# Gathers held back, PSUM output banks set apart, two lists turned later, two decays on another engine

## The chip, the core and the metric

The kernel runs on one core of a Trainium2 chip. The core has a matrix engine (TensorE, PE in the profile; its weight loads are PEld), three others that compute (VectorE, DVE; ScalarE, ACT; GpSimd, POOL), an engine that only issues transfers (SyncE, SP), and sixteen DMA engines that all transfers share, whichever queue they were issued on. Each engine works through its own instructions in the order in which they were written and waits on semaphores for the others. The metric is the device time of one execution in microseconds; less is better.

## What is computed

Linear attention with a decay per head, and then a layer of experts of which each token uses one. Batch 2, 8 heads, 768 steps, head size 64; 8 experts with a hidden size of 1024.

```python
for t in range(S):                                   # attention
    state = gamma * state + outer(k[:, :, t], v[:, :, t])
    y[:, :, t] = scale * einsum(q[:, :, t], state)
x = y, heads side by side                            # 2 x 768 tokens of 512
for each token s of a batch:                         # experts
    fresh = argmax(x @ w_gate)
    e = fresh if s == 0 or sigmoid(x @ w_local) < 0.5 else prev_e
    p = softmax(x @ w_gate)
    out = p[e] * (relu(x @ w1[e]) @ w2[e])
```

## The kernel before

**Attention** goes through six blocks of 128 steps for both batches. Of each block the keys (and for two blocks at a time the queries) are multiplied by powers of the decay (`decay_k`, `decay_q`), turned by TensorE, copied out of PSUM (`k_evac`, `q_evac`), and used for scores, values and a running state. The rows of x go to a DRAM tensor `xs`, each as 1,024 fp16 numbers (512 high parts and 512 low parts; 2,048 bytes). Routing (`fresh`, `choose`, `carry`, `place`) gives for each expert the list of its tokens.

**Experts.** An expert takes up to 256 tokens, as a first list of 128 and a second list with the rest (112 for expert 0 and so on down; sizes in `CAPS`). Expert 0 is the fixed one (`FEW = 1`): its place and its weights are known before routing ends. The other seven come in the order of how many tokens they have, so that their weights can be loaded only when the ranks are known (`experts`). For a list, GpSimd starts a `gather` (an indirect DMA of rows of `xs` into `xg`, of which there are four buffers), TensorE turns it in 8 transposes (`list_transpose`, tokens lt) into a PSUM tile `xtr`, ScalarE or VectorE copies that to `xx` (`list_evac`, le). Then come 8 up products of 12 matmuls each (`up`), the relu in two parts, `hh` by ScalarE and `hl` by VectorE (`relu`, re), and 8 down products (`down`, dn). Expert 0 is done in two rounds, its first list (up.f.0, dn.f.0) and then its second (up.f.1, dn.f.1); its first result is copied out of PSUM by `hold` (ho). After that a loop over the experts 1 to 7 follows, in which the tokens that are written after the word `late` in `ORDER` are worked off one by one.

**Weights** are loaded as 64 transfers of 512 KB (`load_unit`, into a ring of 18 buffers `stg`), four for w1 and four for w2 of an expert, in that order. Each holds two blocks, and each block is split into an fp16 high part `hi` by ScalarE (`split_hi`, token wh) and a low part `lo` by VectorE (`split_lo`, wl).

**The order** of the whole first half is written out by hand in the string `ORDER`, where each token is one step; each engine gets its part in that order. In the stretch of which the prediction speaks most, after the token `reopen`, stand the second list of expert 0 (lt.0.1, le.0.1, up.0.1 to dn.7.1), the two lists of expert 1 (lt.1.0, lt.1.1 and their copies) and the splits of expert 1's w1 (wh and wl). `reopen` closes the PSUM pool of the attention part (tags `big`, 2 x 2 banks, and `one`, 3 banks) and opens the pool `pn` of the expert part, whose tags `xt` (2), `h` (2) and `o` (3) take the banks over. A new tile then waits for what last used its bank. `warm` issues matmuls on zeros, whose results nobody reads.

Of the kernel before, what the change touches and what calls it, by code (L numbers as in the profile page):

```python
# [9 lines left out]
F32 = mybir.dt.float32  # L10
F16 = mybir.dt.float16
# [7 lines left out]
P = 128  # L19
# [39 lines left out]
ls.0 sc.1.0 er.0.0.a er.0.1.v tk.2 rs.0.2.a mk.1.0 Y.1 ek.2.0.a dq.1.0.p ek.2.1.a av.1.0 av.1.1 dq.1.1.v tq.1.0
xh.1 W W tq.1.1 eq.1.0.0.v W eq.1.0.1.a eq.1.1.1.v sc.2.0 eq.1.1.0.a xl.1 st.2 mk.2.0 dk.3.0.p rt.1.1 lo.1 sn.2  # L60
Y.2 ls.1 fr.0 dk.3.1.p fr.0 fr.0 fr.0 sc.2.1 ch.0 ch.0 ch.0 ch.0 tk.3 mk.2.1 kr.0 ek.3.0.a av.2.0 ke.0 ek.3.1.v
av.2.1 dk.4.0.v tr.0 xh.2 st.3 ca.0 xl.2 dk.4.1.p tc.0 rt.1.0 tk.4 er.1.0.a sn.3 sc.3.1 oh.0 rhs.0 dq.2.0.p
ek.4.0.a er.1.1.v co.0 rs.1.2.a mk.3.1 rt.2.0 ek.4.1.a lo.2 er.2.0.a ls.2 tq.2.0 dq.2.1.p pl.0 pl.0 pl.0 sc.3.0
eq.2.0.0.a eq.2.0.1.v mk.3.0 sc.4.0 es.0 tq.2.1 eq.2.1.1.v Y.3 eq.2.1.0.a mk.4.0 av.3.0 dk.5.0.p pl.0 av.3.1
pl.0 pl.0 dk.5.1.v fi.0 xh.3 tk.5 ad.0 sc.4.1 xl.3 ek.5.0.a ek.5.1.a rt.2.1 mk.4.1 lo.3 er.2.1.a rt.3.1 ls.3
sc.5.0 fr.1 wh.a fr.1 fr.1 ch.1 ch.1 kr.1 ch.1 rs.2.2.a ch.1 rt.3.0 wl.v ke.1 er.3.0.a er.3.1.v tr.1 sc.5.1 ca.1
rs.3.2.a mk.5.0 tc.1 wh.a st.4 wh.a oh.1 wl.v wh.a co.1 wl.v wh.a Y.4 es.1 pl.1 wh.a sn.4 wh.a pl.1 rhs.1 pl.1
av.4.0 wh.a pl.1 pl.1 wh.a pl.1 av.4.1 mk.5.1 wh.a fi.1 xh.4 Y.5 ad.1 early wl.v wh.a wl.v av.5.0 wh.a wl.v
av.5.1 wh.a xl.4 wh.a tot xh.5 rc rt.4.0 wl.v lo.4 er.4.0.a xl.5 rt.4.1 er.4.1.a lo.5 ls.4 wl.v rt.5.0 rs.4.2.a
ls.5 fr.2 rt.5.1 fr.2 er.5.0.a fr.2 ch.2 kr.2 wl.v lt.0.0 ch.2 ke.2 ch.2 ch.2 er.5.1.a le.0.0.v tr.2 ca.2 up.0.0  # L70
rs.5.2.a wl.v wh.a tc.2 up.1.0 oh.2 wh.a rhs.2 wl.v co.2 up.2.0 pl.2 es.2 pl.2 pl.2 up.3.0 pl.2 pl.2 up.4.0 pl.2
re.3.0 fi.2 tot up.5.0 rank ad.2 rank up.6.0 rank rank lists dn.0.0 up.7.0 second experts dn.1.0 wl.v re.7.0 W
dn.2.0 ga W dn.3.0 wl.v W ga wl.v W dn.4.0 wl.v W dn.5.0 wl.v W dn.6.0 W dn.7.0 W ho reopen lt.0.1 lt.1.0
le.0.1.v wh.a wh.a wl.v up.0.1 wh.a wl.v up.1.1 le.1.0.a wl.v up.2.1 wh.a lt.1.1 wh.a wl.v up.3.1 wh.a wl.v
up.4.1 re.3.1 up.5.1 le.1.1.a up.6.1 wl.v wh.a up.7.1 wh.a wl.v dn.0.1 wl.v re.7.1 dn.1.1 dn.2.1 dn.3.1 dn.4.1
dn.5.1 dn.6.1 dn.7.1 late ga ga prob prob prob prob prob prob prob prob prob prob sidx pt pl2 so.1 so.0 rest
rest rest
"""

C_ID = 0  # L80
# [40 lines left out]
def moe_kernel(ctx: ExitStack, tc, q, k, v, w_gate, w_local, w1, w2, cst, out):  # L121
# [245 lines left out]
    with ExitStack() as both:  # L367
# [41 lines left out]
        def decay_q(g, b, eng="p"):  # L409

            T["qs", g, b] = ap_.tile([P, 2, H, D], F32, tag="qs", name=f"qs{g}_{b}", bufs=2)
            src = T["q", g, b].rearrange("t h (two d) -> t h two d", two=2)
            for two in range(2):
                eng_[eng[two % len(eng)]].tensor_tensor(
                    T["qs", g, b][:, two].rearrange("t (j r) d -> t r j d", r=2),
                    src[:, :, two].rearrange("t (r j) d -> t r j d", r=2),
                    qtab[:, g, :, two].rearrange("t (r j) -> t r j", r=2).unsqueeze(3).to_broadcast([P, 2, R, D]),
                    ALU.mult,
                )
# [697 lines left out]
```

## Time and profile before

| | us |
|---|---|
| median of 3 runs | 239.21 |
| lowest and highest of them | 237.76 and 239.99 |
| the profiled execution, its own time | 238.68 |
| its span, from the first to the last instruction | 236.9 |
| TensorE busy in the span | 216.7 (91%) |
| VectorE, ScalarE, GpSimd busy | 156.8, 135.4, 55.0 |

The span is 1.8 us shorter than the profiled execution's time. All times in rows are counted from the start of the span. In a list of instructions the number in brackets at the end of a row is the idle time of that engine just before, and what ended it.

### The profile page before, as it was taken

What the parts mean: (1) busy time and instruction counts of PE and PEld (TensorE: products, weight loads), DVE (VectorE), ACT (ScalarE), POOL (GpSimd) and SP (SyncE); (2) the same over time, 40 slices, a digit from 0 to 9 for tenths busy, and PEclk for the clock granted to TensorE, in tenths of its full rate; (3) what the DMA queues carried; (4) which work ended last, traced back from release to release, by engine and by line L of the source; (5) the groups of instructions that cost most, each with busy time, mean ns of one, the idle gap of its engine ahead of it and who ended that gap; (6) DMA issues with size and microseconds to landing.
All of it is one profiled execution on the core that took longest, in us unless ns stands there. A gap on an engine that the chain in (4) does not pass through costs nothing. (4 is left out here: it accounts for less than half of the span.)

```text
span 236.9 us, 7289 instructions
## 1 busy us (share of the span) xinstructions
PE 216.7 (91%) x3056; PEld 178.1 (75%) x3056; DVE 156.8 (66%) x312; ACT 135.4 (57%) x234; POOL 55.0 (23%) x69
## 2 busy tenths in 40 slices
PE   7699898999879859999999999999999999999960
PEld 2489797988779356786589869959969969959940
DVE  2659597889988655188877647756846956967500
ACT  2224415368871257066656676876786886877420
POOL 2334236402102630000111333333021242011030
PEclk9999999999979999999999999999999999999997
DMA  7999999989632699999999896899768622001001
GB/s 168 275 163 266 263 229 256 265 251 400 231 134 79 200 338 358 387 387 386 387 391 335 254 326 209 288 313 291 257 200 284 240 88 74 0 12 44 7 14 44
DMA packets 54565, 53.85 MB, mean 227 GB/s; under 512 B 28516, under 2 KB 34788, under 8 KB 54528
## 3 DMA queue, kind: packets, MB, share of 16 engines
q1 hardware_dynamic: 49952, 43.41, 60.1%
q0 software_dynamic: 2944, 6.78, 8.7%
q10 hardware_dynamic: 1632, 3.15, 3.6%
q8 instruction: 25, 0.41, 0.8%
q14 instruction: 12, 0.10, 0.1%
HBM read 47.03 MB, written 6.69 MB: 227 GB/s over the span
## 5 line engine op out<-in xcount | busy, mean ns | idle before, releaser
L219 DVE SCALAR_TENSOR_TENSOR lo<-stg,hi 128x512 f16<-128x512 f32 x128 | 83.5, 686 | 28.1 <-ACT hi L154 28.0
L154 ACT ACTIVATE hi<-stg 128x512 f16<-128x512 f32 x128 | 73.0, 620 | 6.6 <-DMA stg<-in_moe_w_dram 5.5
L842 PE MATMUL h<-xx,hi 128*128 128x128 f16 (+8 forms) x576 | 72.6, 246 | 0.6 <-DVE xx L156 0.6
L842 PE MATMUL h<-xx,lo 128*128 128x128 f16 (+8 forms) x288 | 67.2, 246 | 0.0
L842 PEld LDWEIGHTS <-hi 128*128 128x128 f16 x576 | 51.5, 98 | 3.6 <-issue 0.7
L926 POOL DMA_INDIRECT out_dram<-ob,sidx x16 | 16.5, 1031 | 114.7 <-ACT ob L925 80.7
L842 PEld LDWEIGHTS <-lo 128*128 128x128 f16 x288 | 28.1, 98 | 0.5
L853 ACT ACTIVATE hh_None<-h 128x512 f16<-128x512 f32 (+6 forms) x28 | 14.7, 526 | 23.8 <-PE h L842 23.8
L854 DVE SCALAR_TENSOR_TENSOR hl_None<-h,hh_None 128x512 f16<-128x512 f32 (+6 forms) x28 | 16.8, 602 | 16.2 <-ACT hh_None L853 15.8
L904 PE MATMUL o<-hi,hh_None 128*128 128x512 f16 (+1 forms) x72 | 25.6, 356 | 0.0
L904 PE MATMUL o<-lo,hh_None 128*128 128x512 f16 (+1 forms) x72 | 25.6, 356 | 0.0
L904 PE MATMUL o<-hi,hl_None 128*128 128x512 f16 (+1 forms) x72 | 25.6, 356 | 0.0
L874 PE MATMUL o<-hh_None,lo 128*128 128x112 f16 (+5 forms) x192 | 21.4, 198 | 0.0
L874 PE MATMUL o<-hh_None,hi 128*128 128x112 f16 (+5 forms) x192 | 21.4, 198 | 0.0
L874 PE MATMUL o<-hl_None,hi 128*128 128x112 f16 (+5 forms) x192 | 21.4, 198 | 0.0
L874 PEld LDWEIGHTS <-hi 128*128 128x128 f16 x384 | 21.3, 97 | 0.0
L764 POOL DMA_INDIRECT xg<-xs,gidx x16 | 17.4, 1088 | 13.8 <-DMA stg<-in_moe_w_dram 4.3
L904 PEld LDWEIGHTS <-hh_None 128*128 128x128 f16 x144 | 13.2, 98 | 9.2
L874 PEld LDWEIGHTS <-lo 128*128 128x128 f16 x192 | 17.5, 98 | 0.0
L475 DVE TENSOR_TENSOR am<-sc,ct 128x1024 f32<-128x1024 f32 x12 | 14.6, 1215 | 2.4 <-PE sc L468 2.3
L154 ACT ACTIVATE xx<-xtr 128x1024 f16<-128x1024 f16 (+6 forms) x14 | 12.2, 871 | 2.7 <-PE xtr L807 2.5
L468 PE MATMUL sc<-qT,kT 64*128 64x128 f32 x192 | 13.6, 282 | 0.0
(148 smaller groups left out, 283.0 us busy)
## 6 DMA issues: line engine op xcount, KB each, us to landing
stg<-in_moe_w_dram SPq DMA_DIRECT2D x64, 512.0 KB, 7.8
k<-in_k_dram SPq DMA_DIRECT2D x12, 256.0 KB, 5.3
q<-in_q_dram SPq DMA_DIRECT2D x6, 512.0 KB, 6.0
v<-in_v_dram SPq DMA_DIRECT2D x12, 256.0 KB, 5.7
xs<-rows ACTq DMA_DIRECT2D x6, 512.0 KB, 5.4
ct<-in_constants_dram SPq DMA_DIRECT2D x1, 264.5 KB, 5.7
xg<-xs,gidx POOLq DMA_INDIRECT x16, 6.1
out_dram<-ob,sidx POOLq DMA_INDIRECT x16, 4.6
```

Source lines behind the costliest of these rows:

```text
L154: nc.scalar.activation(dst, src, AF.Copy, scale=scale)
L219: nc.vector.scalar_tensor_tensor(lo, stg, 2.0**SW, hi, ALU.mult, ALU.subtract)
L468: nc.tensor.matmul(sc[:, r, j], lhsT=T["kT", s][U[r], b, j], rhs=T["qT", s][U[r], b, j], start=True, stop=True, skip_group_check=True,)
L475: nc.vector.tensor_tensor(T["am", s, b].rearrange("p r j t -> p (r j) t"), T["sc", s, b].rearrange("p r j t -> p (r j) t"), tri.unsqueeze( ...
L764: nc.gpsimd.indirect_dma_start(out=xg[:n], out_offset=None, in_=xs[:top, :], in_offset=bass.IndirectOffsetOnAxis(ap=ix[:n, hf * E + e : hf ...
L842: nc.tensor.matmul(ps_[:, f % m, :n_], lhsT=a[:, kk, fs], rhs=xx[:, b_, kk, :n_], start=(n == 0 and f % m == 0), stop=(n == 11), skip_grou ...
L853: nc.scalar.activation(hh[..., :n_], ps_[..., :n_], AF.Relu)
L854: nc.vector.scalar_tensor_tensor(hl[..., :n_], ps_[..., :n_], 0.0, hh[..., :n_], ALU.max, ALU.subtract)
L874: nc.tensor.matmul(PO[e, 1][:, kk, :m], lhsT=a[:, f, kk * P : (kk + 1) * P], rhs=b_[:, f, :m], start=(f == kk == n == 0), stop=(f == KF - ...
L904: T["at"] = nc.tensor.matmul(po[:m], lhsT=a[:, f, :m], rhs=b_[:, f, cols], start=(f == 0 and n == 0), stop=(f == KF - 1 and n == 2),)
L926: nc.gpsimd.indirect_dma_start(out=out[:, :], out_offset=bass.IndirectOffsetOnAxis(ap=LST["sidx"][:m, col : col + 1], axis=0), in_=ob[:m], ...
```

## The change

- **Gathers.** The tokens `ga ga` in the `late` part become `gl gl`, of which each starts two gathers (`later`) and not one, and makes each depend on `T["at"]`, which is at that point the last matmul of dn.7.1. So the gathers of experts 2 and 3 (four lists) start only when the fixed expert is done.
- **Banks.** The tag `o` gets a pool of its own, `po`, that is opened ahead of `pn`.
- **Lists.** lt.1.0 moves from behind lt.0.1 to behind up.3.1, and lt.1.1 from behind up.2.1 to behind up.7.1; their copies le.1.0 and le.1.1 move behind the two relus. `warm.3` is put behind lt.0.1.
- **Queries.** `decay_q` is written for one half at a time. For the first pair of blocks of batch 0, the two halves go from GpSimd to VectorE; one `q_evac` (eq.0.0.1) goes from VectorE to ScalarE; `warm.5` becomes `warm.8`, and `warm.2` is put between tq.0.0 and tq.0.1.
- New code on `XBAR` (`list_dma`, `by_dma`) is never reached, since `XBAR = 8` is the number of experts.

```diff
-dk.0.1.v lk.2.0 lk.2.1 tk.0 warm.5 lq.1.0 lq.1.1 ek.0.0.a ek.0.1.v lv.2.0 dq.0.0.p lv.2.1 lk.3.0 lk.3.1 lv.3.0
+dk.0.1.v lk.2.0 lk.2.1 tk.0 warm.8 lq.1.0 lq.1.1 ek.0.0.a ek.0.1.v lv.2.0 dq.0.0.0.v dq.0.0.1.v lv.2.1 lk.3.0
...
-dn.2.0 ga W dn.3.0 wl.v W ga wl.v W dn.4.0 wl.v W dn.5.0 wl.v W dn.6.0 W dn.7.0 W ho reopen lt.0.1 lt.1.0
-le.0.1.v wh.a wh.a wl.v up.0.1 wh.a wl.v up.1.1 le.1.0.a wl.v up.2.1 wh.a lt.1.1 wh.a wl.v up.3.1 wh.a wl.v
+ga W dn.3.0 wl.v W ga wl.v W dn.4.0 wl.v W dn.5.0 wl.v W dn.6.0 W dn.7.0 W ho reopen lt.0.1 warm.3 le.0.1.v wh.a
+wh.a wl.v up.0.1 wh.a wl.v up.1.1 wl.v up.2.1 wh.a wh.a wl.v up.3.1 lt.1.0 wh.a wl.v up.4.1 re.3.1 le.1.0.a
...
-            to = one("warm")
+            to = bank("xt", 2, F32, (512,), "warm")
...
+        def later():
+
+            ix = gather(*order.pop(0))
+            tc.add_manual_dep(
+                ix, T["at"].ins.name, mybir.DependencyInfo(mybir.DependencyClass.Sync, mybir.DependencyReason.DATA)
+            )
...
-                return pn[0].tile([P, *shape], dtype, tag=tag, name=name, bufs=bufs)
+                return pn[tag != "o"].tile([P, *shape], dtype, tag=tag, name=name, bufs=bufs)
...
-            pn.append(both.enter_context(tc.tile_pool(name="pn", bufs=1, space=PSUM, reuse_waits="tile")))
+            for name in ("po", "pn"):
+                pn.append(both.enter_context(tc.tile_pool(name=name, bufs=1, space=PSUM, reuse_waits="tile")))
...
-            "dn": lambda f, h: down(0, h, f), "so": lambda h: store(0, h), "ho": lambda: hold(0), "ga": lambda: gather(*order.pop(0)),
+            "dn": lambda f, h: down(0, h, f), "so": lambda h: store(0, h), "ho": lambda: hold(0), "ga": lambda: gather(*order.pop(0)), "gl": lambda: (later(), later()),
```

ScalarE before, from the copy of the fixed expert's first result (`ob`) on: `hi` rows are the splits of expert 1's w1, in the order of its four loads (`stg_0` to `stg_3`), `xx` rows the copies of expert 1's two lists, `hh` rows the relus of the fixed expert's second list.

```order
L913 ACTIVATE ob_1552<-o_0_1468 128x512
L154 ACTIVATE hi_1582<-stg_0_1510 128x512 x2
L154 ACTIVATE hi_1582<-stg_1_1517 128x512
L154 ACTIVATE xx_1616<-xtr_0_1571 128x8x128
L154 ACTIVATE hi_1582<-stg_1_1517 128x512
L154 ACTIVATE hi_1582<-stg_2_1523 128x512 x2
L853 ACTIVATE hh_1_1587<-h 128x4x112
L154 ACTIVATE xx_1616<-xtr_1_1632 128x8x128
```

And the same place now.

```order
L935 ACTIVATE ob_1558<-o_0_1474 128x512
L155 ACTIVATE hi_1586<-stg_0_1516 128x512 x2
L155 ACTIVATE hi_1586<-stg_1_1523 128x512 x2
L155 ACTIVATE hi_1586<-stg_2_1529 128x512 x2
L875 ACTIVATE hh_1_1591<-h 128x4x112
L155 ACTIVATE xx_1674<-xtr_0_1648 128x8x128
L155 ACTIVATE hi_1586<-stg_3_1534 128x512 x2
```

The first copy `xx` has moved behind the first relu; the first relu still stands behind both splits of the third load (`stg_2`).

GpSimd before, from the gather of the fixed expert's second list (112 rows) on: the gathers of expert 1 (128 and 128 rows), expert 2 (128 and 112) and the first of expert 3; `out_dram` rows are the scatters of results.

```order
L764 DMA xg_1_1486<-xs,gidx 112x1024
L764 DMA xg_0_1515<-xs,gidx 128x1024
L764 DMA xg_1_1525<-xs,gidx 128x1024
L764 DMA xg_0_1760<-xs,gidx 128x1024
L764 DMA xg_1_1820<-xs,gidx 112x1024
L764 DMA xg_0_1982<-xs,gidx 128x1024
L926 DMA out_dram<-ob,sidx 1536x512 x2
```

And the same place now.

```order
L769 DMA xg_0_1521<-xs,gidx 128x1024
L769 DMA xg_1_1531<-xs,gidx 128x1024
L769 DMA xg_0_1773<-xs,gidx 128x1024
L769 DMA xg_1_1775<-xs,gidx 112x1024
L769 DMA xg_0_1835<-xs,gidx 128x1024
L769 DMA xg_1_1837<-xs,gidx 96x1024
L769 DMA xg_0_1999<-xs,gidx 128x1024
L948 DMA out_dram<-ob,sidx 1536x512 x2
```

Behind expert 1's two gathers there are now the four that wait for the fixed expert (128, 112, 128 and 96 rows), and then the first of expert 4, all ahead of the first scatters.

VectorE near the start, before (`ks`, `qs` decayed keys and queries, `kT`, `qT` copies of turned ones, `c` a cast of constants):

```order
L156 COPY kT_171<-trk_1_144 128x8x64
L414 TENSOR_TENSOR qs_1_185<-q_1_122,ct 128x2x4x64 x2
L156 COPY qT_210<-trq_0_1_189 128x2x256
L156 CAST c_66<-ct 128x512
L156 CAST c_66<-ct 128x128
```

And now:

```order
L157 COPY kT_174<-trk_1_144 128x8x64
L415 TENSOR_TENSOR qs_0_179<-q_0_120,ct 128x2x4x64 x2
L415 TENSOR_TENSOR qs_1_188<-q_1_122,ct 128x2x4x64 x2
L157 CAST c_66<-ct 128x512
L157 CAST c_66<-ct 128x128
```

Two decays came to VectorE and one copy left it.

## Rows read from the trace of the kernel before

**Rows 1.** Who TensorE waited for, from 78 us to the end: total, times, longest.
```profile
PE xtr L807 <- DMA xg<-xs,gidx: 2.6, 2, 1.3
PE xtr L807 <- ACT ob L913: 0.7, 1, 0.7
PE o L904 <- ACT hh L853: 0.3, 1, 0.3
```

**Rows 2.** TensorE in order of time: start, us, what [idle before <- what ended it].
```profile
82.28 0.55 PE L807 MATMUL xtr<-c,xg 112*128 112x112 f16 x8 [0.69 <-ACT ob L913]
84.16 0.62 PE L807 MATMUL xtr<-c,xg 128*128 128x128 f16 x8 [1.33 <-DMA xg<-xs,gidx]
87.78 0.62 PE L807 MATMUL xtr<-c,xg 128*128 128x128 f16 x8 [1.23 <-DMA xg<-xs,gidx]
91.67 0.42 PE L904 MATMUL o<-hi,hh 128*112 128x512 f16 x1 [0.32 <-ACT hh L853]
```

**Rows 3.** ScalarE in order of time in the same stretch.
```profile
81.63 0.60 ACT L913 ACTIVATE ob<-o 128x512 f32<-128x512 f32 x1 [4.01 <-PE o L904]
...
90.04 1.15 ACT L154 ACTIVATE hi<-stg 128x512 f16<-128x512 f32 x2 [2.27 <-DMA stg<-in_moe_w_dram]
91.10 0.52 ACT L853 ACTIVATE hh<-h 128x448 f16<-128x448 f32 x1
```

**Rows 4.** VectorE: the copy of the fixed expert's second list.
```profile
82.87 0.62 DVE L156 COPY xx<-xtr 128x896 f16<-128x896 f16 x1 [2.06 <-PE xtr L807]
```

**Rows 5.** GpSimd in order of time: the three gathers behind expert 1's two.
```profile
80.73 0.95 POOL L764 DMA_INDIRECT xg<-xs,gidx  x1 [0.30 <-issue]
83.10 0.94 POOL L764 DMA_INDIRECT xg<-xs,gidx  x1 [1.43 <-PE xtr L807]
85.06 0.96 POOL L764 DMA_INDIRECT xg<-xs,gidx  x1 [1.01 <-PE xtr L807]
```

**Rows 6.** These and the gather before them, by line: count, first and last issue, landing.
```profile
L764 POOL DMA_INDIRECT xg<-xs,gidx x4: 940/952/1007, 79.4 to 85.1; - x4
...
DMA to landing us min/median/max: 7.3/8.3/8.4
```

**Rows 7.** The third load of expert 1's w1, by line: its issue, time to landing.
```profile
L192 SPq DMA_DIRECT2D stg<-in_moe_w_dram x1: 373/373/373, 79.5 to 79.5; - x1
...
DMA to landing us min/median/max: 10.5/10.5/10.5
```

**Rows 8.** Stretches: length, PE busy (instructions), granted clock, DMA share, GB/s.
```profile
64.00:66.00 2.00, 0.91 (x27) 1.00 0.47 131
66.00:68.00 2.00, 1.90 (x31) 0.67 0.17 62
68.00:70.00 2.00, 1.70 (x16) 0.50 0.57 212
82.00:84.00 2.00, 0.55 (x8) 1.00 0.99 380
88.00:90.00 2.00, 2.00 (x44) 1.00 1.06 312
94.00:96.00 2.00, 2.00 (x11) 1.00 1.06 389
```

**Rows 9.** The start, several engines, in order of time.
```profile
6.73 1.25 PE L733 MATMUL warm<-zero 128*128 128x512 f16 x5
7.65 2.05 POOL L414 TENSOR_TENSOR qs<-q,ct 128x512 f32<-128x512 f32 x2 [5.81 <-DMA q<-in_q_dram]
9.32 1.53 DVE L414 TENSOR_TENSOR qs<-q,ct 128x512 f32<-128x512 f32 x2 [1.75 <-DMA q<-in_q_dram]
10.26 0.63 ACT L154 ACTIVATE qT<-trq 128x512 f32<-128x512 f32 x1 [2.83 <-PE trq L453]
10.94 0.71 PE L453 MATMUL trq<-ct,qs 64*128 64x64 f32 x15 [0.30 <-ACT qT L154]
...
25.85 1.29 DVE L414 TENSOR_TENSOR qs<-q,ct 128x512 f32<-128x512 f32 x2 [2.08 <-DMA q<-in_q_dram]
```

More of the change, by code (lines that the diff above doesn't have):

```diff
@@ L35 @@
 M = E - FEW
+XBAR = 8
 CAPS = (240, 256, 240, 224, 210, 198, 188, 176)
@@ L59 @@
[L59 to L72, printed above, removed]
-dn.2.0 ga W dn.3.0 wl.v W ga wl.v W dn.4.0 wl.v W dn.5.0 wl.v W dn.6.0 W dn.7.0 W ho reopen lt.0.1 lt.1.0
@@ L74 @@
-le.0.1.v wh.a wh.a wl.v up.0.1 wh.a wl.v up.1.1 le.1.0.a wl.v up.2.1 wh.a lt.1.1 wh.a wl.v up.3.1 wh.a wl.v
-up.4.1 re.3.1 up.5.1 le.1.1.a up.6.1 wl.v wh.a up.7.1 wh.a wl.v dn.0.1 wl.v re.7.1 dn.1.1 dn.2.1 dn.3.1 dn.4.1
-dn.5.1 dn.6.1 dn.7.1 late ga ga prob prob prob prob prob prob prob prob prob prob sidx pt pl2 so.1 so.0 rest
-rest rest
+dk.0.1.v lk.2.0 lk.2.1 tk.0 warm.8 lq.1.0 lq.1.1 ek.0.0.a ek.0.1.v lv.2.0 dq.0.0.0.v dq.0.0.1.v lv.2.1 lk.3.0
+lk.3.1 lv.3.0 dq.0.1.0.v dq.0.1.1.v tq.0.0 warm.2 lv.3.1 lk.4.0 lk.4.1 eq.0.0.1.a eq.0.0.0.a tq.0.1 lq.2.0 cast
@@ new lines @@
+lq.2.1 sc.0.0 lv.4.0 eq.0.1.1.a eq.0.1.0.v lv.4.1 lk.5.0 lk.5.1 st.0 lv.5.0 mk.0.0 lv.5.1 W dk.1.0.p sc.0.1
+sn.0.a W W av.0.0 mk.0.1 dk.1.1.p av.0.1 tk.1 xh.0 W W st.1 ek.1.0.v ek.1.1.a xl.0 setup sc.1.1 sn.1 dk.2.0.p
+lo.0 mk.1.1 rt.0.1 rt.0.0 dk.2.1.p ls.0 sc.1.0 er.0.0.a er.0.1.v tk.2 rs.0.2.a mk.1.0 Y.1 ek.2.0.a dq.1.0.0.p
+dq.1.0.1.p ek.2.1.a av.1.0 av.1.1 dq.1.1.0.v dq.1.1.1.v tq.1.0 xh.1 W W tq.1.1 eq.1.0.0.v W eq.1.0.1.a
+eq.1.1.1.v sc.2.0 eq.1.1.0.a xl.1 st.2 mk.2.0 dk.3.0.p rt.1.1 lo.1 sn.2 Y.2 ls.1 fr.0 dk.3.1.p fr.0 fr.0 fr.0
@@ new lines @@
+wl.v wh.a tc.2 up.1.0 oh.2 wh.a rhs.2 wl.v co.2 up.2.0 pl.2 es.2 pl.2 pl.2 up.3.0 pl.2 pl.2 up.4.0 pl.2 re.3.0
+fi.2 tot up.5.0 rank ad.2 rank up.6.0 rank rank lists dn.0.0 up.7.0 second experts dn.1.0 wl.v re.7.0 W dn.2.0
+ga W dn.3.0 wl.v W ga wl.v W dn.4.0 wl.v W dn.5.0 wl.v W dn.6.0 W dn.7.0 W ho reopen lt.0.1 warm.3 le.0.1.v wh.a
+wh.a wl.v up.0.1 wh.a wl.v up.1.1 wl.v up.2.1 wh.a wh.a wl.v up.3.1 lt.1.0 wh.a wl.v up.4.1 re.3.1 le.1.0.a
+up.5.1 up.6.1 wl.v wh.a up.7.1 lt.1.1 wh.a wl.v dn.0.1 wl.v re.7.1 le.1.1.a dn.1.1 dn.2.1 dn.3.1 dn.4.1 dn.5.1
@@ L78 @@
+dn.6.1 dn.7.1 late gl gl prob prob prob prob prob prob prob prob prob prob sidx pt pl2 so.1 so.0 rest rest rest
 """
@@ L407, in load, with decay_q @@
             nc.sync.dma_start(out=t_, in_=src)
-        def decay_q(g, b, eng="p"):
-            T["qs", g, b] = ap_.tile([P, 2, H, D], F32, tag="qs", name=f"qs{g}_{b}", bufs=2)
+        def decay_q(g, b, two, eng="p"):
+            if ("qs", g, b) not in T:
+                T["qs", g, b] = ap_.tile([P, 2, H, D], F32, tag="qs", name=f"qs{g}_{b}", bufs=2)
             src = T["q", g, b].rearrange("t h (two d) -> t h two d", two=2)
[L413 to L419, printed above, removed]
+            eng_[eng].tensor_tensor(
+                T["qs", g, b][:, two].rearrange("t (j r) d -> t r j d", r=2),
+                src[:, :, two].rearrange("t (r j) d -> t r j d", r=2),
+                qtab[:, g, :, two].rearrange("t (r j) -> t r j", r=2).unsqueeze(3).to_broadcast([P, 2, R, D]),
+                ALU.mult,
+            )
         def decay_k(s, b, eng="p"):
@@ L758, in wide, with by_dma @@
             return max(n, HP + 8)
+        def by_dma(n):
+            return -(-n // 16) * 16
         def gather(e, hf, top=NTOK, ix=None):
@@ L762, in gather @@
             ix = LST["gidx"] if ix is None else ix
-            n = wide(rows(e, hf))
-            nc.gpsimd.indirect_dma_start(
+            n = by_dma(rows(e, hf)) if e >= XBAR else wide(rows(e, hf))
+            here = nc.gpsimd.indirect_dma_start(
                 out=xg[:n], out_offset=None, in_=xs[:top, :],
@@ L807, in list_transpose, with list_dma @@
                     nc.tensor.transpose(tr[:, i, kk, :n], xg[:n, c : c + P], id16[:n, :n])
+        def list_dma(e, hf):
+            n = by_dma(rows(e, hf))
+            if hf == 0:
+                XX[e] = mp[0].tile([P, 2, KD, CAP], F16, tag="xx", name=f"xx{e}", bufs=2)
+            nc.scalar.dma_start_transpose(
+                out=XX[e][..., hf * P : hf * P + n].rearrange("p i k t -> p (i k) t"), in_=XG.pop((e, hf))[:n]
+            )
         def list_evac(e, hf, eng="a"):
@@ L985, in moe_kernel @@
                     relu(e, f)
+                if XBAR <= e + 1 < E and f in (1, 3):
+                    list_dma(e + 1, f // 2)
+                if XBAR <= e + 1 and f in (5, 7) and order:
+                    gather(*order.pop(0))
                 split_some(1, 2 * e + 3)
@@ L994, in between @@
                 queue(2 * e + 6)
-                if f == 3 and not last:
+                if f == 3 and e + 1 < min(XBAR, E):
                     list_transpose(e + 1, n)
```

15 lines of the change are left out of this document (12 added, 3 removed).

## The prediction, on record before the result

> **What bounds the kernel now.** I read first who TensorE waited for from 78 us to the end [rows 1]. The reader should see how short the list is: four waits worth naming, 0.69, 1.33, 1.23 and 0.32 us, 3.57 us in sum, and all of them lie between 81.6 and 91.7 us [rows 2]. After 91.67 TensorE always has work, so whatever is won before that moment reaches the end unless something new stops TensorE later. The place to cost is therefore the ten microseconds around the second round of the fixed expert, where the program hands over from routing to experts.
>
> Then I read the other engines in that window, to see what comes next when one of these waits goes. ScalarE matters most [rows 3]. Its first relu of the second round starts at 91.10, and the down products wait for it until 91.67. But the relu itself did not wait for TensorE: it stands in ScalarE's order behind the two splits of the third load of expert 1's w1, and these waited 2.27 us for that load. The load was issued at 79.5 and landed 10.5 us later, at 90.0 [rows 7]. So two chains meet at 91.67: TensorE's own (lists, up products) and third load, splits, relu. From landing to the first down product the second chain takes 91.67 - 90.0 = 1.67 us.
>
> **The change part by part.**
>
> *Banks.* The 0.69 us wait of lt.0.1 for `hold` [rows 2] is a wait for a bank: the transposes need nothing that `hold` makes, and ScalarE's copy from 81.63 to 82.23 [rows 3] ends just before they start at 82.28. With `o` first, `xtr` no longer gets that bank, and the wait goes: -0.69 us. The list itself was there.
>
> *Lists later.* The 1.33 and 1.23 us are waits for expert 1's lists. The first landed at about 84.1 and the second at about 87.75, where TensorE started on them [rows 2]. How fast an up product is: TensorE ran dry at 87.78 - 1.23 = 86.55, after 8 transposes and 3 up products from 84.16, 2.39 us; and from 87.78 to 91.67 - 0.32 = 91.35 it did 8 transposes and 5 up products, 3.57 us. The difference of two up products is 1.18 us, 0.59 each. In the new order lt.0.1 starts at 82.28 - 0.69 = 81.59. Its copy takes 0.62 us on VectorE [rows 4] and is now a bare wait, about 0.7 us with both ends; before, it lay under the wait for the list. `warm.3` lies in this gap: five such matmuls take 1.25 us [rows 9], three 0.65 us by the gap of about 0.21 between starts, so it costs nothing, and at most 0.65 us if the copy were free. Four up products then end at about 85.2, after the first list's landing, and the other four, behind lt.1.0, at about 88.2, after the second's. So both waits go. TensorE is through with all of it at 91.35 - (0.69 + 1.33 + 1.23) + 0.7 = 88.8 us. If the relu were ready, the gain would be 91.67 - 88.8 = 2.87 us. That is the ceiling.
>
> *The relu is not ready.* If the third load still landed at 90.0, the down products would start at 91.67 as before, and the whole gain would turn into one wait of 2.9 us for ScalarE. The copies le.1.0 and le.1.1 now stand behind the relus, which does not help the first relu: le.1.0 filled time in which ScalarE was about to wait for that load anyway. Nor does it hurt: their reader is expert 1's first up product, 24 down matmuls of 512 columns behind the first one, 5.2 us at the 0.21 to 0.22 us of such a matmul (below, `warm`), and in that time ScalarE has two splits (1.15), two relus (0.52 each) and two copies (twice 0.62 or somewhat more [rows 4]), under 4.5 us. So the term that decides is how much sooner the third load lands.
>
> *Gathers put off.* Before, three gathers were started behind expert 1's two, at 80.73, 83.10 and 85.06 [rows 5], and landed 7.3 to 8.4 us later [rows 6]. They carry 128 + 112 + 128 rows of 2,048 bytes, 0.754 MB, through the same DMA engines as the loads. While they are under way the engines move 312 GB/s (88 to 90 us), and 389 from 94 on [rows 8]. Now they start behind the fixed expert's last product, at 90.1 + 5.2 = 95.3 us. What of these bytes had been moved when the third load landed is its advance. Lower end: only the first of the three had landed by 90.0 (0.262 MB at 389 GB/s, 0.67 us). Upper end: all three stood in the way (0.754 MB, 1.94 us). Between: if the second and third moved evenly over the 7.8 us in the middle of those times, 88% and 63% of them were through by 90.0, in sum 0.63 MB, 1.6 us. I take 1.6, since their times to landing are like those of the gathers ahead of them, so they were served beside the loads and not after them. The third load lands at 88.4, the down products start at 90.1, and that is later than TensorE's own 88.8. A wait of 1.3 us for the relu is left, and the gain is 1.6 us.
>
> The Trainium skill, "DMA: Bandwidth & Descriptors", section "Queues, rings and completion order", says that each DMA engine takes turns between the queues that have work, one packet from each. By that rule gathers and loads would share evenly: half of the 2.5 to 3.0 MB that moved from 82 to 90 (at 312 to 380 GB/s [rows 8]) would be gathers, enough for expert 1's two and all three later ones (1.28 MB), and the advance would be the upper 1.94 us, for 237.3 us. The rows speak against quite so even a share, since the last of the three landed only after 92 us.
>
> What the moved gathers cost later: four lists, 464 rows, 0.95 MB, 2.4 us at 389 GB/s, now run for some 8 us from 95 on beside the loads of expert 1's w2 and of expert 2. GpSimd has nothing queued behind them but the first gather of expert 4, which needs a buffer that comes free in expert 1's down products, and scatters of results, which nothing waits for there. The loads run ahead: TensorE has no wait for weights after 78 us at all [rows 1]. A delay of 2.4 us is nothing unless that lead is shorter, and the gathered lists are wanted only behind expert 1's up products, 96 matmuls of 256 columns, which at 0.049 us for 112 columns take 10.8 us. I take 0, with 0 to 0.5 us as bounds.
>
> *The start.* GpSimd took 2.05 us for two halves from 7.65, VectorE takes 1.53 for two [rows 9]. So the first pair is done at 9.2 and not at 9.7, with VectorE back in time for the second pair, whose load lands at 9.32. But the two copies of the turned queries are now both on ScalarE, one behind the other, so the second ends at 9.7 + 2 x 0.6 = 10.9, where the one of before ended too (10.26 + 0.63). The transposes that wait for that copy start at 10.94 [rows 9]. One may start sooner, by up to 0.3 us; three more `warm` matmuls before tq.0.0 end ahead of 8.5, where the decayed half comes. And at 25.85 VectorE waits 2.08 us for a load of queries that nothing computed releases, so what is won or lost at 11 us is gone by then. Bounds -0.3 to 0.3 us, and 0 taken.
>
> **The sum.** 0 at the start, -1.6 us at the first down product, 0 later. The profiled execution would take 238.68 - 1.6 = 237.1 us; it lies 0.5 us under the median of its three runs, and against that median, 239.21, the forecast is **237.6 us**.
>
> **The rivals.**
>
> *The wait only changes its name.* The third load is late for another reason than the three gathers, say because expert 1's own two, which stay, and the loads behind it share the engines with it. Then it lands at 90.0 to 89.3, and the gain is 0 to 0.7 us: 239.2 to 238.5, say 239.0. For it speaks that the loads issued after it also advance in that time; against it, that the first of the three gathers had landed before 90.0, so its bytes did go ahead.
>
> *The full ceiling.* Without the three gathers expert 1's two also land sooner, and the loads by more than bytes say, since the engines moved only 312 GB/s from 88 to 90 and 389 later [rows 8]. If the third load lands by 87.1, ScalarE is no longer the last and the gain is 2.87 us: 236.3 us.
>
> *Slower: the clock falls.* Before, TensorE's idle time came in pieces. Now the up products run through and a single gap stands ahead of the down products. What the granted clock can do is seen at 64 to 66 us: PE was busy 0.91 of 2 us, and then the granted clock was 0.67 in the mean from 66 to 68 and 0.50 from 68 to 70 [rows 8], the 1.2 GHz level instead of 2.4: 3.3 us at half. But from 82 to 84, with 0.55 busy of 2 us, it stayed at 1.00. It decides when the third load lands no sooner: then the gap, with the 8 transposes ahead of it, lasts from about 88.2 to 91.67, 3.5 us, where the longest so far (81.59 to 84.56) was 3.0. If the clock then stays at half for 3.3 us, as it did there, half of that is lost, 1.65 us, with nothing gained: 240.9 us.
>
> *The moved gathers do collide later.* If ScalarE comes to a split whose load is late, every relu behind it is late too, as at 90.04. It would give back most of the 1.6 us, up to 2.4: 239.2 to 240.0 us, say 239.5. The short list of waits speaks against it.
>
> **How the numbers follow.** Forecast, gains from 0.7 to 2.4 us: 0.58. The wait changes its name: 0.20. Full ceiling: 0.15. Clock: 0.04. Later collision: 0.03. A measurement of this kernel cannot tell less than about 1%, 2.4 us, from no change; the three runs before alone span 2.2 us. Faster by over 1% is the ceiling's case almost whole (0.13) and about a fifth of the forecast's by the scatter of medians (0.12): 0.25. Slower by over 1% is a third of the clock's case and a little of the collision and of scatter: 0.04. The rest, 0.71, is within 1%. The range reaches from the ceiling with 0.7 us of scatter, 235.6, to no gain with 0.6 us of scatter, 239.8; the clock's case is outside.
>
> **What the changed profile would show.** The wait for `ob` and both waits for `xg` gone; lt.0.1 at 81.6, a wait of under 0.1 us or a run of `warm` in the gap of the copy, and the up products in one run to about 88 us. Then one wait of PE for ACT `hh`, of 1 to 1.5 us, and the first down product at about 90. The third load's time to landing at 9 us and not 10.5. Four gathers in a row on GpSimd from about 95 us, and no new wait of TensorE after them. The start unchanged from 26 us on. Wrong would be: a third load at 90 us (then the time stays), a granted clock under 1.00 between 88 and 96, or waits of ScalarE for loads after 95 us.

## The result, and the profile after

The changed kernel takes 237.23 us (median of 14 runs, 235.88 to 239.55), the kernel before in the same session 239.66 us (14 runs, 237.76 to 242.0). The ratio is 0.9906, with an interval from 0.9878 to 0.9934. It leaves out the one run of each kernel that was over 1.5% above its fastest; without these the medians are 237.21 and 239.46, so the change is 2.25 us or 0.94% faster. The forecast was 237.6 us, or 0.9933 of the 239.21 us it started from. The profiled execution took 237.24 us with a span of 235.5 us, where the one before had 238.68 and 236.9.

Who TensorE waited for in the profile after, from 78 us to the end (total, times, longest), answers to [rows 1]:

```profile
PE o L926 <- ACT hh L875: 1.1, 1, 1.1
PE xtr L820 <- issue: 0.3, 1, 0.3
```

The waits for `ob` and for both lists are gone. One wait for the first relu is left, and a pause of 0.3 us much later. TensorE in order of time (start, us, what, idle before), against [rows 2]:

```profile
81.71 0.56 PE L820 MATMUL xtr<-c,xg 112*128 112x112 f16 x8
82.11 0.81 PE L734 MATMUL warm<-zero 128*128 128x512 f16 x3
82.99 0.26 PE L864 MATMUL h<-xx,hi 128*128 128x112 f16 x2
...
85.34 0.61 PE L820 MATMUL xtr<-c,xg 128*128 128x128 f16 x8
...
88.15 0.61 PE L820 MATMUL xtr<-c,xg 128*128 128x128 f16 x8
89.87 0.42 PE L926 MATMUL o<-hi,hh 128*112 128x512 f16 x1 [1.11 <-ACT hh L875]
...
95.37 0.38 PE L864 MATMUL h<-xx,hi 128*128 128x256 f16 x2
...
130.51 0.44 PE L820 MATMUL xtr<-c,xg 128*128 128x128 f16 x5 [0.32 <-issue]
```

The first transposes no longer wait for a bank, `warm` fills the gap of the list's copy, and all eight up products run through with the two turned lists between them. TensorE is done with them at 89.87 - 1.11 = 88.76. ScalarE shows what it then waits for (compare [rows 3]):

```profile
81.91 0.60 ACT L935 ACTIVATE ob<-o 128x512 f32<-128x512 f32 x1 [4.02 <-PE o L926]
84.16 1.15 ACT L155 ACTIVATE hi<-stg 128x512 f16<-128x512 f32 x2 [1.65 <-DMA stg<-in_moe_w_dram]
85.85 1.15 ACT L155 ACTIVATE hi<-stg 128x512 f16<-128x512 f32 x2 [0.54 <-DMA stg<-in_moe_w_dram]
88.24 1.15 ACT L155 ACTIVATE hi<-stg 128x512 f16<-128x512 f32 x2 [1.25 <-DMA stg<-in_moe_w_dram]
89.30 0.52 ACT L875 ACTIVATE hh<-h 128x448 f16<-128x448 f32 x1
```

The chain is that of before, third load, two splits, relu, only earlier: the splits of the third load start at 88.24 where they started at 90.04. SyncE's queue issued that load at 79.9 (first and last start are the same), so the load landed 8.3 us after its issue or sooner, where [rows 7] has 10.5:

```profile
L193 SPq DMA_DIRECT2D stg<-in_moe_w_dram x1: 292/292/292, 79.9 to 79.9; - x1
```

GpSimd in the same stretch, against [rows 5]: after the second list of expert 1 nothing is started until the fixed expert's last product, then four gathers start in a row.

```profile
79.69 1.02 POOL L769 DMA_INDIRECT xg<-xs,gidx  x1 [0.30 <-issue]
95.81 0.95 POOL L769 DMA_INDIRECT xg<-xs,gidx  x1 [15.10 <-PE o L926]
97.06 0.94 POOL L769 DMA_INDIRECT xg<-xs,gidx  x1 [0.30 <-issue]
98.30 0.95 POOL L769 DMA_INDIRECT xg<-xs,gidx  x1 [0.30 <-issue]
99.56 0.92 POOL L769 DMA_INDIRECT xg<-xs,gidx  x1 [0.30 <-issue]
```

How much of it reaches the end is seen by two rows of each trace, expert 1's first up product and the last product of the program. Before:

```profile
97.29 0.38 PE L842 MATMUL h<-xx,hi 128*128 128x256 f16 x2
228.36 0.27 PE L904 MATMUL o<-hi,hl_None 128*128 128x256 f16 x1
```

After, the first is the row at 95.37 above, 1.92 us sooner, and the other is 1.44 us sooner:

```profile
226.92 0.27 PE L926 MATMUL o<-hi,hl_None 128*128 128x256 f16 x1
```

The copy `ob` itself starts 0.28 us later in this profile than before (81.91, 81.63), through the part that the change hardly touches. Over all profiles of this study it starts anywhere from 80.2 to 83.1 us. So kernels are compared below by distances from the start of this copy, which no step of the second round can move. What comes behind the second round is far steadier: from expert 1's first up product to the last product of the program it is 228.36 - 97.29 = 131.07 us before the change, 131.06 or 131.07 in ten more of the twelve profiles, and 131.55 in the profile after. So what the kernels differ by lies between `ob` and expert 1's first up product. A distance still comes from a single execution. The changed kernel has two profiles (after, a1_again), and their first down products differ by 0.27 us; the kernel of e1 has two as well, and these differ by 0.47 us there and by 1.77 us at expert 1's first up product.

### The profile page after: what moved, and what is told of

It reads as the page before. It is cut to its first block, busy times and chain, and to the rows that moved or that the text cites. A ratio compares the mean times of both kernels' runs of the same rounds, so it can differ in the third digit from the quotient of the medians.

```text
span 235.5 us, 7303 instructions
## 1 busy us (share of the span) xinstructions
PE 216.6 (92%) x3064; PEld 177.4 (75%) x3064; DVE 157.9 (67%) x313; ACT 135.8 (58%) x235; POOL 53.7 (23%) x67
## 5 line engine op out<-in xcount | busy, mean ns | idle before, releaser
L948 POOL DMA_INDIRECT out_dram<-ob,sidx x16 | 16.4, 1022 | 80.8 <-ACT ob L947 47.3
L769 POOL DMA_INDIRECT xg<-xs,gidx x16 | 18.2, 1135 | 46.3 <-PE xtr L820 19.5
L424 POOL TENSOR_TENSOR ks<-k,ct 128x512 f32<-128x512 f32 x8 | 8.3, 1051 | 26.9 <-DMA k<-in_k_dram 26.0
```

The costliest lines, as they stand in the source:

```text
L424: eng_[eng].tensor_tensor(T["ks", s, b].rearrange("t (j r) d -> t r j d", r=2), T["k", s, b].rearrange("t (r j) d -> t r j d", r=2), ktab[ ...
L769: here = nc.gpsimd.indirect_dma_start(out=xg[:n], out_offset=None, in_=xs[:top, :], in_offset=bass.IndirectOffsetOnAxis(ap=ix[:n, hf * E + ...
L948: nc.gpsimd.indirect_dma_start(out=out[:, :], out_offset=bass.IndirectOffsetOnAxis(ap=LST["sidx"][:m, col : col + 1], axis=0), in_=ob[:m], ...
```

## The experiments

Theory: the second round of the fixed expert ends with whichever comes last, TensorE's own work (lists, up products) or the third load with its splits and relu. The gathers delay the load, the old order of the lists delays TensorE, and only both edits together gain. Rivals: the new order of lists and banks alone makes the gain; or holding the gathers back alone does; or it is made elsewhere, at the start. The kernels left nothing out of the computation.

| kernel | ratio to before (95%) | splits of third load | first down product | expert 1's first up |
|---|---|---|---|---|
| before | 1 | 8.41 | 10.04 | 15.66 |
| after | 0.9906 (0.9878 to 0.9934) | 6.33 | 7.96 | 13.46 |
| a1_again | 0.9936 (0.9906 to 0.9967) | 6.59 | 8.23 | 13.72 |
| e1_not_held | 1.0052 (1.0023 to 1.0081) | 8.19 | 9.82 | 16.62 |
| e12_not_held_again | 1.0019 (0.9981 to 1.0058) | 7.72 | 9.35 | 14.85 |
| e11_not_held_gap_filled | 1.0013 (0.9972 to 1.0054) | 8.34 | 9.97 | 15.47 |
| e2_only_held | 0.9990 (0.9955 to 1.0025) | 6.72 | 11.51 | 16.70 |
| e4_lists_as_before | 0.9940 (0.9903 to 0.9976) | 6.74 | 9.50 | 14.69 |
| e3_banks_as_before | 0.9918 (0.9874 to 0.9962) | 6.68 | 8.31 | 13.81 |
| e7_start_only | 1.0010 (0.9970 to 1.0049) | 8.54 | 10.17 | 15.67 |
| e6_relu_first | 0.9840 (0.9809 to 0.9872) | 6.65 | 6.68 | 11.86 |
| e10_relu_first_not_held | 0.9899 (0.9841 to 0.9958) | 8.40 | 6.68 | 12.89 |

The three last columns are us from the start of `ob` in the one profile of each kernel, read as in the rows above (after: 88.24, 89.87 and 95.37, each less 81.91). a1, e1, e2 and e6 shared one chip, e3, e4, e7 and e10 another, e12 and e11 a third; each ratio is to the kernel before on the same chip.

The third load itself explains its column. It is issued 2.0 to 2.1 us ahead of `ob` in all twelve profiles. From issue to landing it then takes 8.6 to 8.8 us in the profiles that hold the gathers back (in after, where the trace gives no landing, 8.3 or less by the splits) and 9.8 to 10.6 us in the six that don't. The two loads issued ahead of it are no later for the gathers: where the traces give their landings, these are 5.2 to 5.8 us and 6.1 to 7.3 us after issue, with no gap between the two groups. The third load in a1 and the same one in e1:

```profile
L193 SPq DMA_DIRECT2D stg<-in_moe_w_dram x1: 373/373/373, 81.0 to 81.0; - x1
DMA to landing us min/median/max: 8.6/8.6/8.6
...
L193 SPq DMA_DIRECT2D stg<-in_moe_w_dram x1: 373/373/373, 81.0 to 81.0; - x1
DMA to landing us min/median/max: 10.2/10.2/10.2
```

**a1_again.** The changed kernel once more, no edit.

> The changed kernel once more, as the yardstick of this chip. From the start of the copy of the fixed expert's first result (ob) to the first down product of its second list: 8.0 us as in its first profile (10.0 before). Both theories: ratio 0.988 to 0.993 to the kernel before.

Ratio 0.9936, a wait for the relu of 1.3 us. That is a little less gain than expected, and its interval overlaps the first one; the change is worth 0.6 to 0.9%.

**e1_not_held.** The changed kernel, but the later gathers don't wait for the fixed expert's last product.

```diff
             ix = gather(*order.pop(0))
-            tc.add_manual_dep(
-                ix, T["at"].ins.name, mybir.DependencyInfo(mybir.DependencyClass.Sync, mybir.DependencyReason.DATA)
-            )
```

> The changed kernel with its gathers not held back: same tokens, but the four gathers no longer depend on the fixed expert's last product. Theory 1 (the third load of expert 1's w1 decides, and the gathers delay it): the load lands 8.0 to 8.5 us after ob's start as before (6.3 in the changed kernel), the first down product comes 9.5 to 10.1 us after ob's start, TensorE waits 2.5 to 3 us for ACT hh, ratio 0.997 to 1.002. Theory 2 (banks and list order make the gain, and gathers are bystanders): first down product 7.8 to 8.3 us after ob's start, ratio 0.988 to 0.993.

Banks, lists and start are all in, and the kernel is slower than before, 1.0052. Against a1 on the same chip the dependence alone is worth 3.19 us in the medians (239.78, 236.59). The list of TensorE's waits after 78 us has one entry:

```profile
PE o L923 <- ACT hh L872: 3.0, 1, 3.0
```

And ScalarE, where the third load comes:

```profile
91.28 1.15 ACT L155 ACTIVATE hi<-stg 128x512 f16<-128x512 f32 x2 [3.34 <-DMA stg<-in_moe_w_dram]
```

The waits for the lists have become one wait for the relu, since the third load is as late as before. That is what the prediction's rival has, in which the wait only changes its name; here the gathers make it so. But 3.0 us of wait in place of 3.57 doesn't explain a loss. In this profile TensorE's granted clock, by stretches (length, PE busy, granted clock, DMA share, GB/s), falls behind the wait, to the 1.2 GHz level of the two:

```profile
90.00:92.00 2.00, 0.00 (x0) 1.00 1.05 312
92.00:94.00 2.00, 1.09 (x3) 0.68 1.04 382
94.00:96.00 2.00, 2.00 (x7) 0.50 1.06 348
```

The 24 down products take 16.62 - 9.82 = 6.80 us, in the profile after 13.46 - 7.96 = 5.50. So 1.3 us went that way in this execution. Whether it does so in most, the two kernels of the third chip were to tell.

**e12_not_held_again** is the same kernel as e1.

> The kernel of e1 (changed, gathers not held back) as the yardstick of this chip. If the clock is what makes it slower than the kernel before: first down product 9.8 us after ob's start, a granted clock well under 1.00 in the 4 to 8 us behind it, 6.5 to 7 us from the first down product to expert 1's first up product, ratio 1.002 to 1.008.

**e11_not_held_gap_filled** is e1 with eleven matmuls of zeros behind the last turned list, on a free bank of `o`, so that TensorE's wait is filled but for 0.75 us.

```diff
-up.5.1 up.6.1 wl.v wh.a up.7.1 lt.1.1 wh.a wl.v dn.0.1 ...
+up.5.1 up.6.1 wl.v wh.a up.7.1 lt.1.1 warm.11.o wh.a wl.v dn.0.1 ...
```

> The kernel of e1 with eleven matmuls on zeros (2.4 us, in an output bank that is free, so that they wait for nothing) put on TensorE in its wait of 3.0 us for the third load's relu. Theory (the long single wait lets the granted clock fall, and that is why e1 was slower than the kernel before): the first down product comes at 9.8 us after ob's start as in e1, the clock stays at 1.00, from there to expert 1's first up product it takes 5.5 us and not 6.8, ratio 0.997 to 1.001, 0.4 to 0.6% below e1 on the same chip. Rival (the clock falls in e1's profile by chance, and the rest of e1 is slower for another reason): ratio as e1's, 1.003 to 1.008.

The same kernel as e1 has a wait nearly as long in e12's profile, as TensorE's order of time shows:

```profile
90.14 0.42 PE L923 MATMUL o<-hi,hh 128*112 128x512 f16 x1 [2.50 <-ACT hh L872]
```

This time the granted clock, by stretches as above, stays at 2.4 GHz:

```profile
88.00:90.00 2.00, 0.00 (x0) 1.00 1.00 338
90.00:92.00 2.00, 1.84 (x8) 1.00 1.06 389
92.00:94.00 2.00, 2.00 (x11) 1.00 1.05 345
```

Its down products take 5.50 us, and so do those of e11, with the gap filled. The ratios 1.0019 and 1.0013 can't be told apart. So the clock may cost 1.3 us in some executions, but that it is why the new order without the hold gains nothing isn't shown; the theory that it is, which e11 was to bear out, fell. What the three profiles do show fits a gain of about nothing: the first down product stands at 9.35 to 9.97, before at 10.04, and expert 1's first up product at 16.62, 14.85 and 15.47, before at 15.66. That e1 came out slower by half a per cent stays open.

**e2_only_held.** The kernel before, with the last two `ga ga` made `gl gl`, `later()` as in the change, and nothing else.

```diff
-dn.5.1 dn.6.1 dn.7.1 late ga ga prob ...
+dn.5.1 dn.6.1 dn.7.1 late gl gl prob ...
```

> The kernel before with the gathers held back and nothing else. Theory 1: the third load lands about 6.3 us after ob's start as in the changed kernel, but TensorE's own chain with both list waits is now the last: the second list lands at about 5.5 us, 8 transposes and 5 up products (3.6 us) follow, first down product 9.0 to 9.8 us after ob's start, ratio 0.996 to 0.999. Theory 2 (gathers are bystanders): 10.0 us, ratio 1.000. Theory 3 (the gathers alone make the gain): 8.0 us, ratio 0.990.

The load comes 1.7 us sooner (6.72, 8.41), and the time doesn't move. TensorE in order of time:

```profile
82.37 0.55 PE L815 MATMUL xtr<-c,xg 112*128 112x112 f16 x8 [0.69 <-ACT ob L921]
83.88 0.62 PE L815 MATMUL xtr<-c,xg 128*128 128x128 f16 x8 [0.95 <-DMA xg<-xs,gidx]
88.21 0.62 PE L815 MATMUL xtr<-c,xg 128*128 128x128 f16 x8 [1.94 <-DMA xg<-xs,gidx]
```

The second list still stops TensorE ahead of five up products, at 6.49 us from `ob` (before 6.15). From there to the first down product it is 11.51 - 6.49 = 5.02 us in this profile, where [rows 2] have 91.35 - 87.78 = 3.57, because the granted clock was 0.50 from 90 to 92. At full clock the first down product would stand at 6.49 + 3.57 = 10.06 by this estimate, as before. With the old order the load is no longer what comes last, so its 1.7 us show in no median.

**e4_lists_as_before.** The change, but with the list tokens of the second round in the old order, without `warm`.

```diff
-reopen lt.0.1 warm.3 le.0.1.v ... up.3.1 lt.1.0 ... up.4.1 re.3.1 le.1.0.a up.5.1 up.6.1 ... up.7.1 lt.1.1 ... re.7.1 le.1.1.a
+reopen lt.0.1 lt.1.0 le.0.1.v ... up.1.1 le.1.0.a ... up.2.1 ... lt.1.1 ... up.4.1 re.3.1 up.5.1 le.1.1.a up.6.1 ... up.7.1 ... re.7.1
```

> The changed kernel with the stretch from lt.0.1 to dn.7.1 in the order of before (expert 1's lists turned early, no warm.3). Theory 1: the load lands as in the changed kernel, some 6.5 us after ob's start, but the second list comes only then too, and 3.6 us of transposes and up products stand behind it; waits for xg of 2.5 us or more return, first down product 9.5 to 10.2 us after ob's start, ratio 0.997 to 1.002. Rival (the list order is worth nothing, and the held gathers bring the lists sooner as well): 8.0 to 8.5 us, ratio 0.990 to 0.995.

Both waits for lists are back, and no wait for the relu is left; the load comes at 6.74, the first down product only at 9.50.

```profile
82.87 0.62 PE L820 MATMUL xtr<-c,xg 128*128 128x128 f16 x8 [2.12 <-DMA xg<-xs,gidx]
86.49 0.62 PE L820 MATMUL xtr<-c,xg 128*128 128x128 f16 x8 [1.23 <-DMA xg<-xs,gidx]
```

By distances it wins 15.66 - 14.69 = 0.97 us of the change's 1.9 to 2.2. Its ratio, 0.994, says 1.4 us with an interval from 0.6 to 2.3. That is more than expected for it, and it can't be told from that of the whole change on another chip; the rows, not the ratios, show that the lists come last here. On its own chip e3, whose lists are in the new order, is 0.94 us faster in the medians (235.94, 236.88) and 0.88 by distances, though the two intervals overlap.

So "only both together" is too strong. The change without its order of lists still wins half of the gain by distances, while e2, which lacks the banks and the start as well, shows none in its medians. One difference between the two is seen in the rows: the fixed expert's list is turned from 80.19 on here, 0.20 us ahead of `ob` at 80.39, and in e2 from 82.37 on, 0.65 us behind `ob`. How much of the 0.97 us this makes was not tested.

**e3_banks_as_before.** The change, with all tiles of the experts in one pool again.

```diff
-                return pn[tag != "o"].tile([P, *shape], dtype, tag=tag, name=name, bufs=bufs)
+                return pn[0].tile([P, *shape], dtype, tag=tag, name=name, bufs=bufs)
...
-            for name in ("po", "pn"):
+            for name in ("pn",):
```

> The changed kernel with the tag o back in one PSUM pool with xt and h. Theory 1 (third load decides): the wait of 0.7 us for ob returns, TensorE's own chain ends 0.7 us later, and that is still under its wait of 1.1 to 1.3 us for ACT hh; first down product 7.9 to 8.3 us after ob's start, hh wait 0.4 to 0.6 us, ratio 0.990 to 0.995 like the changed kernel. Rival (each wait of TensorE counts by itself): 8.7 us, ratio 0.993 to 0.998.

The time is that of the change. The wait for `ob` isn't back at the list, as was expected; a shorter one stands at the matmuls of zeros. The up products behind them start 0.2 us later by distance than in the profile after, which lies under the wait of 1.2 us for the relu:

```profile
80.97 0.81 PE L734 MATMUL warm<-zero 128*128 128x512 f16 x3 [0.29 <-ACT ob L935]
```

Output banks first are worth nothing measurable beside the rest. What the 0.69 us wait of the list would cost the changed kernel isn't measured, since it didn't come back. Why the wait hit `warm` and not the list is argued only: one more `warm` tile at the start shifts which bank each later tile gets in turn. That e7, which has this tile but no `po` pool, shows no wait for `ob` either agrees with it.

**e7_start_only.** The kernel before, with the change's start alone: `dq` by halves on VectorE, `warm.8`, `warm.2`, both copies on ScalarE.

```diff
-dk.0.1.v lk.2.0 lk.2.1 tk.0 warm.5 ... dq.0.0.p ... dq.0.1.v tq.0.0 ... eq.0.0.1.v eq.0.0.0.a
+dk.0.1.v lk.2.0 lk.2.1 tk.0 warm.8 ... dq.0.0.0.v dq.0.0.1.v ... dq.0.1.0.v dq.0.1.1.v tq.0.0 warm.2 ... eq.0.0.1.a eq.0.0.0.a
```

> The kernel before with the changed start only (decays of the first queries by VectorE, the copy on ScalarE, warm.8 and warm.2). Theory 1: nothing, ratio 0.998 to 1.002; first scores of block 0 within 0.3 us of 11.4 us, and from the load of queries at 25.9 us on the same. Rival (the start costs or gives something that the first stretch carries on): ratio off by 0.4% or more.

Ratio 1.0010, third load and first down product as before within 0.13 us: the start is worth nothing that can be measured. But the fixed expert's list is turned without a wait for `ob` (which starts at 82.06 in this profile), with all expert tiles in one pool as before:

```profile
81.86 0.56 PE L808 MATMUL xtr<-c,xg 112*128 112x112 f16 x8
84.41 0.62 PE L808 MATMUL xtr<-c,xg 128*128 128x128 f16 x8 [1.99 <-DMA xg<-xs,gidx]
```

So the edits at the start are enough to take away the 0.69 us wait. The granted clock fell here behind the wait for the first list, to 0.73 from 84 to 86 and 0.50 from 86 to 88. The first down product doesn't show it, since it waits for the relu in any case (0.42 us).

**e6_relu_first.** The change, with the first relu of the second round moved ahead of the splits of the third load, and the second relu ahead of those of the fourth.

```diff
-... up.2.1 wh.a wh.a wl.v up.3.1 lt.1.0 wh.a wl.v up.4.1 re.3.1 le.1.0.a up.5.1 up.6.1 wl.v wh.a up.7.1 lt.1.1 wh.a wl.v dn.0.1 wl.v re.7.1 le.1.1.a
+... up.2.1 wl.v up.3.1 re.3.1 lt.1.0 wh.a wl.v up.4.1 up.5.1 up.6.1 wh.a up.7.1 lt.1.1 re.7.1 wl.v le.1.0.a wh.a wl.v dn.0.1 wh.a wl.v le.1.1.a
```

> The changed kernel with the two relus of the fixed expert's second list put ahead of the splits of the third and of the fourth load on ScalarE and VectorE; nothing else is moved but the tokens around them. Theory 1: the wait of 1.1 us for ACT hh goes, the first down product comes 6.8 to 7.0 us after ob's start, and the time falls by another 1.0 to 1.2 us, ratio 0.984 to 0.988. Rival (the wait only passes to the low part hl on VectorE, or to expert 1's first up product, whose list copy or weight splits come later): first down product 6.9 us, but expert 1's first up product no sooner than 13.5 us after ob's start, ratio as the changed kernel's.

234.04 us against 238.16 before and 236.59 of a1 on the same chip: it beats both, and its interval lies clear of a1's. ScalarE in order of time:

```profile
84.14 1.15 ACT L154 ACTIVATE hi<-stg 128x512 f16<-128x512 f32 x2 [0.68 <-DMA stg<-in_moe_w_dram]
85.20 0.52 ACT L874 ACTIVATE hh<-h 128x448 f16<-128x448 f32 x1
86.94 1.15 ACT L154 ACTIVATE hi<-stg 128x512 f16<-128x512 f32 x2 [1.22 <-DMA stg<-in_moe_w_dram]
87.99 0.52 ACT L874 ACTIVATE hh<-h 128x448 f16<-128x448 f32 x1
```

And TensorE's first down product:

```profile
86.97 0.38 PE L925 MATMUL o<-hi,hh 128*112 128x512 f16 x1
```

The first relu is through before the third load's splits begin, and TensorE has no wait at all after 78 us. The first down product follows the last turned list at once, 1.55 us sooner than in a1 (8.23, 6.68); the 24 products then take 5.18 us instead of 5.49. That is 1.86 us in all. The medians say 2.55 us. The difference between these two is within the intervals and wasn't followed further.

**e10_relu_first_not_held.** e6 without the dependence that e1 takes away (the same three lines).

> The kernel with the relus first (e6) with the gathers not held back. Theory 1: the first relu no longer stands behind the third load, so the first down product still comes 6.9 us after ob's start; but the second relu and the splits of the third and fourth loads are later by the 1.8 us that the gathers cost, so expert 1's first up product comes 0.7 to 1.7 us later than in e6 (12.6 to 13.6 us after ob's start, 11.9 in e6), ratio 0.987 to 0.991. Rival (with the relus first the gathers are hidden): 11.9 us, ratio 0.984.

The first down product stands where it does in e6, but the third load is late again (8.40), and now its relu, the second of the round, stops the down products halfway:

```profile
90.20 0.42 PE L922 MATMUL o<-hi,hh 128*112 128x512 f16 x1 [0.47 <-ACT hh L871]
```

Expert 1 starts 12.89 - 11.86 = 1.03 us later than in e6. So holding the gathers still pays with the relus first, through the same load. This rests on the rows; the ratios of e6 and e10, 0.9840 and 0.9899, point the same way, but they are from two chips and their intervals overlap.

## Why the prediction was right

The forecast of 1.6 us and its mechanism held (2.25 us measured, 1.5 us by the ratio of a1): the third load decides, holding the gathers brings it sooner, and the new order keeps TensorE's own work ahead of it. The parts were less exact than the sum.

*Banks.* The wait of lt.0.1 went, as forecast, but the reason given, the pool of its own for `o`, isn't what it takes: e7 has no such pool and no such wait, nor does the list wait in e3. The sum didn't count the 0.69 us apart, since the load came last.

*Lists later.* Both waits went, and TensorE was through at 88.76, forecast 88.8. That the two agree to 0.04 us is luck, since `ob` starts 0.28 us later in this profile; counted from `ob` it is 6.85, forecast 88.8 - 81.63 = 7.17. e4 shows the price of leaving the lists where they were: they then come last.

*The relu.* From the splits of the third load to the first down product it took 89.87 - 88.24 = 1.63 us, forecast 1.67; the remaining wait was 1.11 us (1.3 in a1), forecast 1.3.

*Gathers put off.* In the one profile after, the load came 8.41 - 6.33 = 2.08 us sooner, which looks like the upper bound. All profiles together say otherwise. The six kernels that hold the gathers back (after, a1, e2, e3, e4, e6) have 6.33 to 6.74, mean 6.62; the six that don't (before, e1, e7, e10, e11, e12) have 7.72 to 8.54, mean 8.27. The difference is 1.65 us, and 1.6 was taken. This is not quite the case of the forecast: e1, e10, e11 and e12 have the new order of lists, and their third gather starts later (4.3 us after `ob` in each of them, 3.4 before the change). The two kernels with the gathers as before (before, e7) give 8.48 - 6.62 = 1.86 us, so 1.6 may have been somewhat small. The Trainium skill, "DMA: Bandwidth & Descriptors", section "Queues, rings and completion order", says that each DMA engine takes turns between the queues for which it has work, a packet from each. That the shares of the bytes are even is the prediction's own step, and its estimate by it, 1.94 us, lies above both means. From issue to landing the load took 8.6 us in a1, forecast 9.

*Later cost.* The 1.92 us at expert 1's start are still 1.92 at expert 2's first up product (119.58 before, 117.66 after), and 1.44 are left at the end. The 0.48 us between are lost at the pause at 130.51, whose cause isn't known. They lie within the bounds of 0 to 0.5. The other five profiles that hold the gathers back have no such loss (131.07 us from expert 1's first up product to the last), so it is no fixed cost of the four gathers: 0 was right. The *start* cost nothing, as taken.

The rivals: that the wait only changes its name happens if the gathers aren't held (e1, e11, e12), which is what the three edits have to do with each other. The full ceiling wasn't reached by the change. e6 passes it by another way: its first down product comes 10.04 - 6.68 = 3.36 us sooner than before, where the ceiling was 2.87, so the ceiling was taken too low: TensorE's own work, forecast to end 7.17 us after `ob`, was through by 6.68. The prediction had the first relu standing behind the splits but did not ask what it would be worth to move it. The clock did fall behind a single long wait once (e1), and the price, 1.3 us, is near the 1.65 forecast for that case, but the change with its wait of 1.1 to 1.3 us showed no fall after 82 us.

## What to carry to other kernels

Where two chains meet at one instruction, price both to their ends: here neither the gathers held back alone (e2, 0.999) nor the rest of the change without them (e1, e11, e12, 1.0013 to 1.0052) gained anything in the medians, and together they were worth 0.6 to 0.9%. When an engine works in order, look at what stands ahead of the instruction that is waited for: a relu whose operand is long there, behind a conversion that waits for a load, costs its wait, and to move it ahead was worth more than the change (e6). A gather for work that is tens of microseconds away is not free if it shares the DMA engines with a load that is wanted now: here three of them made it 1.9 us later (before and e7 against the six with the gathers held).

## What the runs showed of the hardware that was not expected

TensorE's granted clock in one and the same part of the program falls in some executions and not in others. Between 66 and 70 us, behind stretches in which PE has little to do, [rows 8] show 0.67 and 0.50 before the change, and a1 0.86 and 0.50; the profile after has

```profile
66.00:68.00 2.00, 0.98 (x24) 1.00 0.44 127
68.00:70.00 2.00, 1.26 (x23) 1.00 0.66 251
```

and the same holds for the profiles of e2, e3, e4, e6, e10, e11 and e12. e1 and e7 fell there too (0.71 and 0.50 between 68 and 72, 0.97 and 0.50 between 66 and 70). The copy `ob` behind it starts at 81.6 to 83.1 us in the four profiles with the fall (mean 82.5) and at 80.2 to 81.9 us in the eight without (mean 80.8), so the fall may make some of the scatter, but not all of it. What decides whether the clock falls isn't known from these runs.

In the second round it is the same. The clock fell behind waits of TensorE of 1.94 us (e2), 1.99 us (e7) and 2.97 us (e1), and stayed at 1.00 behind waits of 2.12 us (e4) and 2.50 us (e12), the last in the same kernel as e1. So the length of one wait doesn't tell.

All this is a scatter of one to two microseconds in single executions, as large as the change itself. It is the reason to read a change of this size by distances from a fixed instruction rather than by the two spans.
